# Moving the statistics, norms and transposes of four token tiles between groups of matmuls

## The chip, the cores and the metric

The kernel runs on one core of a Trainium2 chip. The core has engines with instruction queues of their own, each worked off strictly in order: TensorE (matrix multiplies; PE in the profile, its weight loads PEld), VectorE (DVE), ScalarE (ACT), GpSimd (POOL) and SyncE (SP), which here only issues DMAs. They meet through semaphores: an instruction waits until a producer on another engine, or a DMA, has counted up. The metric is the device time of one execution in microseconds (us), as the median of several runs.

## The reference

A transformer block in bf16 on x of 2048 tokens by 1024: a layer norm, a linear attention with 32 heads, an output projection and a residual; then a second layer norm, a gated FFN with a hidden width of 3584, and a residual.

```python
n  = layernorm(x)                       # no scale, no bias, eps 1e-5
q, k, v = split(n @ wqkv)               # 32 heads of 32
phi = lambda t: where(t > 0, t + 1, exp(t)) + 1e-6
kv  = einsum("hsd,hse->hde", phi(k), v) # sums over all tokens
z   = einsum("hsd->hd", phi(k))
o   = (phi(q) @ kv) / (phi(q) @ z + 1e-6)
h   = x + o @ wo
m   = layernorm(h)
out = h + (relu(m @ W_gate) * (m @ W_up)) @ W_down
```

The change lies in the first stage: layer norm, k, v and the sums over tokens.

## The kernel before

**Tiles.** The 2048 tokens are 16 tiles `st` of 128. In turn a tile is loaded (`load_x1`, into a ring of four places, so tile 8 takes the place of tile 4, tile 12 that of tile 8), gets its mean and variance, is normalised on VectorE (`ln1_norm`: line 970, or 914 for tiles whose statistics came from VectorE), and is transposed by a DMA on SP (`T1d`, issued at line 641) into `xnT`, where the contracted dimension lies on the partitions. `T1d(st)` issues the load of tile st + 4 behind its transpose; `T1d(st, False)` doesn't.

**Two ways to the statistics.** `ln1_stats` and `ln1_steps` run on VectorE: two `bn_stats` (line 859), one aggregate (864), one add (868), then a power on POOL (871). `ln1_steps` returns these as four steps. `ln1_stats_act` runs on ScalarE with accumulating activations (line 885): a mean over 1024 elements, and squares, which come as two halves, `q0` and `q`; small steps on POOL follow each (891, 900, 906, 909). In the code `m6, q6a, q6b` are the mean and the two halves for tile 6, and `m9`, `late_q` hold those of later tiles until a place calls them.

**Groups of seven products.** Pairs of tiles are multiplied by a fast scheme of the Strassen-Winograd kind (`sgroup`): the 2 by 2 blocks of tokens and contraction, times the 2 by 2 blocks of contraction and output columns, take seven products of four 128x128x512 matmuls in place of eight. It needs sums of weight blocks (`w_sums`, line 1068, queues `twk`, `twv`, `twq`) and, for each pair p of tiles, four sums of its transposed blocks, `x_sums(p)` (line 1093, results Sx3, Sx1, Sx2, Sx4 in this order). The order in a group is P1, P7 (uses Sx3), P6 (Sx2), P2, P5 (Sx1), P4, P3 (Sx4). ScalarE copies the first bank of a product to a second one to be added to (`fk1` behind P1, for P6; `fk2` behind P6, for P5; all at line 850) and keeps two banks as `s7` and `sc`. A k group applies phi to its results: an exp on ScalarE (925), two steps on VectorE (929, 932), for two of the four blocks with a sum before (1187). A v group copies two blocks on ScalarE (1254) and sums two on VectorE (1248).

The groups run in the order k0, v2, k1, v3, k2, v4, k3, ...: `k_group(p)` and then `v_group(p + 2)`, where the number is the pair of tiles (v of pairs 0 and 1 comes from single products, `v_piece`, at the start). So v4 needs `x_sums(4)`, of tiles 8 and 9. Between P7 and P6 of k1 and k2, and before P3 of the later v groups, stand the small matmuls that sum over tokens (`kvacc`).

**What sets the order.** Nothing plans at run time: the program is written out in one order, and each engine's queue is its share of that order. `sgroup` calls `hook(i)` at seven places: 1 behind P1 and `fk1`, 2 behind P7, 3 behind P6 and `fk2`, 4 behind P2, 5 behind P5 (in v2 before the sum of that place, elsewhere behind it), 6 behind P4, 7 at the end. A hook first runs what the group before left in `pend[i]` (the rest of its phi, or its sums) and then the function that the caller gave. For k groups these come from `kv_hooks` and the loop at line 2353, for v groups from `v3`, `v5`, `v6`, `v7` at lines 2366 to 2409, where p is 0 for v2, 1 for v3, 2 for v4.

In the kernel before, the mean of tile 6 (`m6`) is called between two single products ahead of k0, its first half square (`q6a`) at k0's hook 3, its second at v2's hook 5, where tiles 6 and 7 are also normalised and transposed, with the loads of tiles 10 and 11 behind. Tile 8 gets its statistics at v3's hook 2 and its norm and transpose at hook 3; tile 9 its norm and transpose at hook 5.

Of the kernel before, what the change touches and what calls it, by code (L numbers as in the profile page):

```python
# [132 lines left out]
def bass_sequential_preLN__linear_attn_block__glu_gated_reglu__prompt_kernel(  # L133
# [71 lines left out]
    with es:  # L205
# [6 lines left out]
        NX1 = 4  # L212
# [423 lines left out]
        def dma(slot, dst_ap, src_ap, name, reads=(), writes=(), eng="sp"):  # L636
            return PL.add(eng, lambda e: e.dma_start(dst_ap, src_ap), reads=reads, writes=writes, slot=slot,  # L637
                          name=name)
# [5 lines left out]
        def load_x1(st, split=False):  # L644
            i = st % NX1
            if split:
                for c in range(NBC):
                    dma(sl_x1h[c], x1[:, i, c * BCH:(c + 1) * BCH], xv[st * P:(st + 1) * P, c * BCH:(c + 1) * BCH],
                        "ld_x1_%d_%d" % (st, c), writes=[B_x1[i][c]], eng=("sp", "act")[c])
            else:  # L650
                dma(sl_x1[i], x1[:, i, :], xv[st * P:(st + 1) * P, :], "ld_x1_%d" % st, writes=B_x1[i])
# [224 lines left out]
        def ln_stats(src_full, src_chunk_bufs, name):  # L876
            k, steps = ln_stats_steps(src_full, src_chunk_bufs, name)
            for f_ in steps:
                f_()
            return k  # L880
# [69 lines left out]
        def ln1_stats(st):  # L950
            i = st % NX1
            ln1_k[st] = ln_stats(x1[:, i, :], B_x1[i], "ln1_%d" % st)

        def ln1_steps(st):
            i = st % NX1
            ln1_k[st], steps = ln_stats_steps(x1[:, i, :], B_x1[i], "ln1_%d" % st)
            return steps

        def ln1_stats_act(st, split=False):
            i = st % NX1  # L960
            k = len(ln1_a) % 3
            ln1_a[st] = k
            return act_stats(x1[:, i, :], B_x1[i], xn[:, st % NXN, :], B_xn[st % NXN], s1[:, k, :], B_s1[k],
                             "ln1_%d" % st, split)

        def ln1_norm(st):
            i = st % NX1
            if st in ln1_a:
                k = ln1_a[st]
                PL.add("dve", lambda e: e.tensor_scalar(out=xn[:, st % NXN, :], in0=x1[:, i, :], scalar1=s1[:, k, 0:1],  # L970
                                                        scalar2=s1[:, k, 2:3], op0=ALU.subtract, op1=ALU.mult),
                       reads=B_x1[i] + [B_s1[k][0], B_s1[k][2]], writes=[B_xn[st % NXN]], name="ln1_%d_norm" % st)
            else:
                ln_norm_dve(ln1_k.pop(st), x1[:, i, :], B_x1[i], xn[:, st % NXN, :], B_xn[st % NXN], "ln1_%d" % st)
            if st in (2, 3):
                load_x1(st + NX1)
# [36 lines left out]
        def T1d(st, load=True):  # L1013
            k = st % NXN
            dma_t(sl_tx[k], xnT[:, :, st * P:(st + 1) * P], xn[:, k, :], "T1d_%d" % st, reads=[B_xn[k]],
                  writes=B_xnT[st])
            if load and st + NX1 < NST:
                load_x1(st + NX1)
# [36 lines left out]
        def v_copy(b, st, j):  # L1055
            sc, rd = (1.0, []) if st >= 2 else (rstd[:, v_k[st], :], [B_rstd[v_k[st]]])
            PL.add("act", lambda e: e.activation(out=v_out(st, j), in_=gw(bank(b)), func=ACTF.Identity, scale=sc),  # L1057
                   reads=[B_bank[b]] + rd, writes=[B_v[st % NV][j]], name="v_%d_%d" % (st, j))
# [22 lines left out]
        def x_sums(p, part=None):  # L1081
            def xb(k, t):
                st = 2 * p + t
                return xnT[:, k * KH:(k + 1) * KH, st * P:(st + 1) * P]

            def s(i):
                return Sx(i)[:, :, p * P:(p + 1) * P]

            def bx(k, t):
                return [B_xnT[2 * p + t][k]]  # L1090

            def add(i, in0, in1, op, reads):
                PL.add("dve", lambda e: e.tensor_tensor(out=s(i), in0=in0, in1=in1, op=op), reads=reads,  # L1093
                       writes=[B_Sx[i][p]], name="Sx%d_%d" % (i + 1, p))

            if part != 1:
                add(2, xb(0, 0), xb(0, 1), ALU.subtract, bx(0, 0) + bx(0, 1))
            if part == 0:
                return
            add(0, xb(0, 1), xb(1, 1), ALU.add, bx(0, 1) + bx(1, 1))  # L1100
            add(1, s(0), xb(0, 0), ALU.subtract, [B_Sx[0][p]] + bx(0, 0))
            add(3, xb(1, 0), s(1), ALU.subtract, [B_Sx[1][p]] + bx(1, 0))
# [72 lines left out]
        pend = {}  # L1175
# [1115 lines left out]
        T1d(4)  # L2291
        m6, q6a, q6b = ln1_stats_act(6, True)
        v_piece(3, 0)
        m6()
        twv.pop(0)()
        ln1_norm(5)
        T1d(5)
# [3 lines left out]
        b31 = v_piece(3, 1, copy=False)  # L2301
# [4 lines left out]
        def kv_hooks(p, nq):  # L2306

            sq = []
            A, B = 2 * p + 6, 2 * p + 7

            def k1():
                if p > 1 and A < NST:
                    ln1_stats(A)
                for _ in range(nq[0]):
                    twq.pop(0)()

            def k5():
                if p < 2:
                    x_sums(p + 2)
                elif p + 2 < NP_:  # L2320
                    x_sums(p + 2, 0)
                if p == 0:
                    m_, q0_, q_ = ln1_stats_act(B, True)
                    m_()
                    sq.extend([q0_, q_])
                while p == 1 and m9:
                    m9.pop(0)()
                while p > 0 and len(late_q) > (p == 1):
                    late_q.pop(0)()

            def k6():
                if p == 0:
                    twv.pop(0)()
                elif 1 < p < NP_ - 2:
                    x_sums(p + 2, 1)
            return {1: k1, 5: k5, 6: k6}, sq

        def norm(st):
            if st < NST:
                ln1_norm(st)  # L2340
                T1d(st)

        def norms(p):
            norm(2 * p)
# [8 lines left out]
        for p in range(NP_):  # L2353
            nq = NQ.get(p, (0, 0))
            hooks, sq = kv_hooks(p, nq)
            if p == 0:
                hooks[1], hooks[3] = lambda: v_copy(b31, 3, 1), q6a
            if p == NP_ - 1:
                hooks[7] = lambda: kvaccs(NP_ - 2)
            if p in (1, 2):  # L2360
                hooks[2] = lambda p=p: kvaccs(p - 1)
            k_group(p, hooks)
            if p + 2 < NP_:
                late = []

                def v3(p=p, sq=sq, late=late):
                    if p == 0:
                        x_sums(1)
                        return
                    if p == 1:  # L2370
                        late_q.pop(0)()
                    norm(2 * p + 6)
                    if 2 * p + 9 < NST:
                        m_, q0_, q_ = ln1_stats_act(2 * p + 9, True)
                        late += [m_, q_]
                        if p == 1:
                            late.append(q0_)
                        else:
                            q0_()

                def v5(p=p, sq=sq, late=late):
                    if p == 0:
                        for f_ in [q6b] + sq:
                            f_()
                        ln1_norm(6)
                        T1d(6, False)
                        ln1_norm(7)
                        T1d(7, False)
                        load_x1(6 + NX1)
                        load_x1(7 + NX1)  # L2390
                        return
                    norm(2 * p + 7)
                    for f_ in late[2:]:
                        f_()
                    if late:
                        late[0]()
                        late_q.append(late[1])

                def v6(p=p, nq=nq):
                    if p > 1:  # L2400
                        kvaccs(p)
                    for _ in range(nq[1]):
                        twq.pop(0)()

                def v7(p=p):
                    if p == 0:
                        m_, q0_, q_ = ln1_stats_act(9, True)
                        m9.append(m_)
                        late_q.extend([q0_, q_])
                vh_ = {3: v3, 5: v5, 6: v6, 7: v7}  # L2410
                if p == 1:
                    vh_[2] = lambda: ln1_stats(8)
                v_group(p + 2, vh_)
        assert not twq and not twv and not twk
        for i in range(ND2):
# [2 lines left out]
        for r in range(2):  # L2418
            for ct in range(NG // 2):
                hooks = {}  # L2420
# [268 lines left out]
```

## Time and profile before

| what | before |
|---|---|
| median of three runs | 715.29 us (714.87 to 715.64) |
| the profiled execution | 714.91 us, of which the span from first to last instruction is 713.1 us |
| TensorE busy | 707.2 us, 99% of the span |
| VectorE, ScalarE, POOL busy | 606.4, 411.5, 141.6 us |
| granted TensorE clock | 1.000 |
| x tile load by SP, issue to landing | 4.0 us (median) |
| DMA transpose of a tile (line 641), issue to landing, 8 to 130 us | 2.7 / 3.7 / 7.7 us (least, median, most) |

Times inside the execution are counted from the span's start. In a line of the timeline the columns are start, duration, engine, source line, operation, tiles written and read, shape, count, and in brackets the idle time of the engine before it and what ended it. In a line of waits they are who waited, for whom, the total, the number and the longest. In the chain of the work that ended last they are start, duration and what.

### The profile page before, as it was taken

Reading aid. Unit: us, or ns where it says so; the run is one execution under the profiler, and the core shown is the slowest. Engines: PE = TensorE matmul, PEld = TensorE weight load, DVE = VectorE, ACT = ScalarE, POOL = GpSimd, SP = SyncE. Lnnn points to the kernel's source line nnn. Section 1 sums busy time; section 2 is a strip of 40 time slices with the busy share of each in tenths; the row PEclk is TensorE's granted clock in tenths of the full one; section 3 lists DMA queues with packets and bytes.
Section 4 is the critical chain, followed back from the end, with each engine's and each line's share of the span. In section 5 each row is a group of like instructions: output and inputs, shape, how many; then the busy total and the mean of one; then the engine's idle time right before and its main releaser. Section 6 shows DMA issues by size and latency. Waiting matters only on the chain.

```text
span 713.1 us, 13262 instructions
## 1 busy us (share of the span) xinstructions
PE 707.2 (99%) x5039; PEld 392.8 (55%) x5039; DVE 606.4 (85%) x974; ACT 411.5 (58%) x741; POOL 141.6 (20%) x206
## 2 busy tenths in 40 slices
PE   9999999999999999999999999999999999999998
PEld 4443444444444455555554658865555555547887
DVE  6988867899878899999998787888889888988985
ACT  4897756764973687878786411046666767633010
POOL 3221100114983223132312001310000000000331
PEclk9999999999999999999999999999999999999999
DMA  9863245114999799999897989995343544267997
GB/s 297 262 99 82 33 115 167 44 30 93 236 195 286 224 333 304 317 249 297 260 296 238 279 241 321 313 222 161 97 133 111 149 116 127 76 206 256 320 316 188
DMA packets 195104, 144.21 MB, mean 202 GB/s; under 512 B 53984, under 2 KB 172512, under 8 KB 195040
## 3 DMA queue, kind: packets, MB, share of 16 engines
q1 hardware_dynamic: 190048, 138.77, 67.2%
q0 software_dynamic: 4032, 3.67, 3.6%
q10 hardware_dynamic: 960, 0.92, 0.4%
q8 instruction: 40, 0.66, 0.4%
q14 instruction: 24, 0.20, 0.1%
HBM read 98.76 MB, written 32.51 MB: 184 GB/s over the span
## 4 chain that ended last, share of the span: by engine, by line
PE 92%; DMA 3%; DVE 1%; issue 1%; ACT 1%; SPq 0%; POOL 0%; DVEq 0%; POOLq 0%
PE ps L845 92%; DMA RAB<-RXH 2%; DMA RE<-in_A_x_dram 1%; ACT RXH L885 1%; SPq L637 0%; DVE RWG L1093 0%; DVE RE L1971 0%; DVE st L859 0%; DVE RXH L970 0%; ACT RE L1057 0%; DVE RWG L1911 0%; DVE RE L1248 0%; DVE RX L1187 0%; ACT RX L850 0%; POOL s L909 0%
## 5 line engine op out<-in xcount | busy, mean ns | idle before, releaser
L850 ACT ACTIVATE ps<-ps 128x512 f32<-128x512 f32 (+1 forms) x263 | 133.1, 517 | 181.4 <-PE ps L845 137.1
L845 PE MATMUL ps<-RC,RO 128*128 128x512 f16 x616 | 147.0, 370 | 0.0
L845 PEld LDWEIGHTS ps<-RC,RO 128*128 128x128 f16 x616 | 60.0, 98 | 53.2 <-ACT ps L850 1.2
L850 ACT ACTIVATE RE<-ps 128x512 f32<-128x512 f32 (+3 forms) x106 | 63.8, 627 | 32.1 <-PE ps L845 18.0
L845 PE MATMUL ps<-RC,RWG 128*128 128x512 f16 x320 | 81.1, 380 | 0.7 <-ACT ps L850 0.6
L845 PE MATMUL ps<-RH,RWG 128*128 128x512 bf16 (+1 forms) x348 | 77.7, 349 | 0.0
L1980 POOL DMA_DIRECT2D out_dram<-RX x20 | 17.9, 1258 | 271.5 <-DVE RX L1971 218.4
L845 PE MATMUL ps<-RH,RO 128*128 128x512 bf16 (+1 forms) x256 | 65.3, 380 | 0.0
L1710 DVE TENSOR_TENSOR RE<-ps,RE 128x1024 bf16<-128x1024 f32 (+1 forms) x42 | 44.0, 1047 | 18.2 <-PE ps L845 18.1
L845 PE MATMUL ps<-RW,RAB 128*128 128x256 f16 (+3 forms) x374 | 56.0, 303 | 0.0
L845 PEld LDWEIGHTS ps<-RH,RWG 128*128 128x128 bf16 x348 | 33.9, 98 | 35.3 <-ACT ps L850 0.2
L845 PE MATMUL ps<-RAB 128*128 128x512 bf16 (+3 forms) x250 | 52.9, 349 | 0.0
L845 PEld LDWEIGHTS ps<-RC,RWG 128*128 128x128 bf16 (+1 forms) x320 | 30.0, 98 | 34.6 <-ACT ps L850 5.8
L845 PEld LDWEIGHTS ps<-RW,RAB 128*128 128x128 f16 (+1 forms) x374 | 36.4, 98 | 16.2 <-DVE RAB L1422 0.5
L1971 DVE TENSOR_TENSOR RE<-ps,RE 128x512 f32<-128x512 f32 x44 | 30.2, 687 | 14.4 <-PE ps L845 11.8
L1710 DVE TENSOR_TENSOR RAB<-ps,RE 128x1024 bf16<-128x1024 f32 x28 | 34.2, 1223 | 7.3 <-PE ps L845 6.6
L1722 ACT ACTIVATE RAB<-RAB 128x1024 bf16<-128x1024 bf16 x28 | 29.5, 1053 | 18.9 <-DVE RAB L1710 18.9
L1710 DVE TENSOR_TENSOR RAB<-RAB,RE 128x1024 bf16<-128x1024 bf16 x56 | 37.3, 686 | 3.1 <-ACT RE L850 2.8
L1576 DVE TENSOR_TENSOR RO<-RWG 128x1024 f16<-128x1024 bf16 x54 | 38.9, 721 | 0.0
L845 PEld LDWEIGHTS ps<-RH,RO 128*128 128x128 f16 (+1 forms) x256 | 24.4, 98 | 24.6 <-ACT RX L850 1.5
L1576 DVE TENSOR_TENSOR RO<-RWG,RO 128x1024 f16<-128x1024 bf16 x54 | 37.8, 700 | 0.0
L845 PEld LDWEIGHTS ps<-RAB 128*128 128x128 bf16 (+1 forms) x250 | 24.3, 98 | 21.9 <-ACT RAB L988 0.3
(212 smaller groups left out, 1294.8 us busy)
## 6 DMA issues: line engine op xcount, KB each, us to landing
RWG<-in_B_W_gate_dram SPq DMA_DIRECT2D x28, 512.0 KB, 5.6
RWG<-in_B_W_up_dram SPq DMA_DIRECT2D x28, 512.0 KB, 5.0
RW<-l_scr SPq DMA_DIRECT2D x20, 448.0 KB, 5.4
RW<-in_B_W_down_dram SPq DMA_DIRECT2D x14, 512.0 KB, 6.3
t_scr<-RW SPq DMA_DIRECT2D x14, 512.0 KB, 4.4
l_scr<-RX SPq DMA_DIRECT2D x7, 1024.0 KB, 7.9
RE<-l_scr SPq DMA_DIRECT2D x15, 448.0 KB, 5.4
RW<-t_scr SPq DMA_DIRECT2D x13, 448.0 KB, 5.6
```

The source lines that it names most:

```text
L845: lambda e: e.matmul(out_ap, lhsT, rhs, start=start, stop=stop, skip_group_check=skip),
L850: PL.add("act", lambda e: e.activation(out=dst, in_=src, func=func), reads=reads, writes=writes, name=name)
L885: PL.add("act", lambda e: e.activation(out=junk[:, c0:c1], in_=src[:, c0:c1], func=func, scale=scale, accum_out=sv[:, col:col + 1]), reads ...
L1576: PL.add(eng, lambda e: e.tensor_tensor(out=tb(j, u), in0=f0(u), in1=f1(u), op=ALU.subtract), reads=[B_w[i + x] for x in r] + ([B_T[k + x] ...
L1710: PL.add("dve", lambda e: e.tensor_tensor(out=dst, in0=in0, in1=in1, op=op), reads=reads, writes=writes, name=name)
L1722: PL.add("act", lambda e: e.activation(out=d, in_=d, func=ACTF.Relu), reads=[], writes=db, name=name)
L1971: PL.add(eng, lambda e: e.tensor_tensor(out=dst, in0=in0, in1=in1, op=op), reads=reads, writes=writes, name=name)
L1980: PL.add("pool", lambda e: e.dma_start(dst, src, accum_op=ALU.add), reads=[bsrc], writes=[B_hscr[st]], slot=sl, name="acc_%d_%d" % (st, dh))
```

## The change

It moves existing work to other places of the written order; no arithmetic is changed or left out. `m6` goes from ahead of k0 to k0's hook 5, in front of tile 7's mean, and `q6a` from k0's hook 3 to v2's hook 3. Tile 8's statistics go from v3's hook 2 to v2's hook 5: the two `bn_stats` between norms 6 and 7, the aggregate and the rest behind the loads of tiles 10 and 11. Tile 8's norm and transpose go from v3's hook 3 to its hook 2; tile 9's from the function at hook 5 into the list `pend[5]`, between the exp and the two VectorE steps of k1's last phi. The loads of tiles 12 and 13, each of which stood behind its transpose (8 and 9), now follow at v3's hook 5, behind both.

```diff
@@ -2291,7 +2291,6 @@
         T1d(4)
         m6, q6a, q6b = ln1_stats_act(6, True)
         v_piece(3, 0)
-        m6()
         twv.pop(0)()
         ln1_norm(5)
         T1d(5)
@@ -2320,6 +2319,7 @@
                 elif p + 2 < NP_:
                     x_sums(p + 2, 0)
                 if p == 0:
+                    m6()
                     m_, q0_, q_ = ln1_stats_act(B, True)
                     m_()
                     sq.extend([q0_, q_])
@@ -2335,10 +2335,10 @@
...
-        def norm(st):
+        def norm(st, load=True):
             if st < NST:
                 ln1_norm(st)
-                T1d(st)
+                T1d(st, load)
...
@@ -2354,7 +2354,7 @@
...
             if p == 0:
-                hooks[1], hooks[3] = lambda: v_copy(b31, 3, 1), q6a
+                hooks[1] = lambda: v_copy(b31, 3, 1)
...
@@ -2365,11 +2365,13 @@
 
                 def v3(p=p, sq=sq, late=late):
                     if p == 0:
+                        q6a()
                         x_sums(1)
                         return
                     if p == 1:
                         late_q.pop(0)()
-                    norm(2 * p + 6)
+                    if p > 1:
+                        norm(2 * p + 6)
...
@@ -2384,12 +2386,21 @@
                             f_()
                         ln1_norm(6)
                         T1d(6, False)
+                        s8 = ln1_steps(8)
+                        s8[0]()
+                        s8[1]()
                         ln1_norm(7)
                         T1d(7, False)
                         load_x1(6 + NX1)
                         load_x1(7 + NX1)
+                        s8[2]()
+                        s8[3]()
                         return
-                    norm(2 * p + 7)
+                    if p > 1:
+                        norm(2 * p + 7)
+                    if p == 1:
+                        load_x1(2 * p + 6 + NX1)
+                        load_x1(2 * p + 7 + NX1)
...
@@ -2409,7 +2420,8 @@
                 vh_ = {3: v3, 5: v5, 6: v6, 7: v7}
                 if p == 1:
-                    vh_[2] = lambda: ln1_stats(8)
+                    vh_[2] = lambda: norm(8, False)
+                    pend[5].insert(1, lambda: norm(9, False))
                 v_group(p + 2, vh_)
```

## The prediction

> **What bounds the kernel now.** I read the page first (busy times, then the chain that ended last), then TensorE's waits, then the timeline of each engine from 19 to 64 us, where every edit lies.
>
> ```profile
> PE 92%; DMA 3%; DVE 1%; issue 1%; ACT 1%; SPq 0%; POOL 0%; DVEq 0%; POOLq 0%
> ...
> PE ps L845 <- POOL RXH L618: 1.4, 1, 1.4
> PE ps L845 <- DVE RWG L1093: 0.9, 2, 0.4
> PE ps L845 <- ACT ps L850: 0.6, 1, 0.6
> ...
> 58.13 615.17 PE ps L845 x4316
> ```
>
> The chain is TensorE, from 58.13 us on 615 us of it without a break. So a microsecond that TensorE gains before 58 us comes out at the end, unless something new stops it. Its waits in the whole run are three: the start, one on ScalarE, two on VectorE's `x_sums` (L1093). Their places, in the timeline of TensorE:
>
> ```profile
> 23.17 1.03 PE L845 MATMUL ps<-RC,RWG 128*128 128x512 f16 x4
> 24.76 1.04 PE L845 MATMUL ps<-RC,RWG 128*128 128x512 f16 x4 [0.56 <-ACT ps L850]
> ...
> 55.21 1.03 PE L845 MATMUL ps<-RAB 128*128 128x512 bf16 x4
> 56.65 1.04 PE L845 MATMUL ps<-RW,RWG 128*128 128x512 f16 x4 [0.41 <-DVE RWG L1093]
> 58.13 1.02 PE L845 MATMUL ps<-RW,RWG 128*128 128x512 f16 x4 [0.45 <-DVE RWG L1093]
> 59.00 1.03 PE L845 MATMUL ps<-RAB 128*128 128x512 bf16 x4
> ```
>
> A product of four matmuls shows 1.03 us, but products without a wait start 0.87 us apart (58.13 to 59.00), as the last matmul's end overlaps the next. I therefore measure a stall from start to start, less 0.87: k0's P6 loses 24.76 - 23.17 - 0.87 = 0.72; v4's P7 loses 0.57 and its P6 0.61. A fourth shows only this way: in k1, P7 starts at 36.18 and P6, behind two `kvacc`, at 37.95, 1.77 apart, where k2 (49.29 to 50.89) takes 1.60: 0.17. Together 2.07 us is all that could be had here.
>
> The other two engines around them:
>
> ```profile
> 23.07 1.05 ACT L885 ACTIVATE RXH<-RE 128x1024 bf16<-128x1024 bf16 x1
> 24.02 0.20 ACT L885 ACTIVATION_READ_ACCUMULATOR RXH<-RE 128x1 f32 x1
> 24.11 0.59 ACT L850 ACTIVATE ps<-ps 128x512 f32<-128x512 f32 x1
> ...
> 28.66 0.68 DVE L1187 TENSOR_TENSOR RX<-ps,RX 128x512 f32<-128x512 f32 x1
> 29.36 0.77 DVE L1093 TENSOR_TENSOR RWG<-RAB 128x512 f16<-128x512 bf16 x2
> ...
> 50.59 1.24 SPq L641 DMA_TRANSPOSE RAB<-RXH  x1
> ...
> 56.17 0.42 DVE L1093 TENSOR_TENSOR RWG<-RAB 128x512 f16<-128x512 bf16 x1 [1.10 <-DMA RAB<-RXH]
> ```
>
> The mean of tile 6 (23.07) stands before the fork copy `fk1` (24.11) that k0's P6 waits for. VectorE has no idle time at all from 22.08 to 37.7. And the transpose of tile 9, issued at 50.59, lands at 56.15 (5.56 us), which is what VectorE and, through it, v4 wait for.
>
> **Edit 1: mean and squares of tile 6.** *k0.* P1 ends at 23.17 + 0.16 = 23.33, so with the mean (1.04 us to the next start) gone `fk1` runs 23.43 to 24.01 and P6 starts at 24.07, behind P7 (24.04): the 0.72 is gone, less 0.03. The half square `q6a` (0.61) goes from behind `fk2` as well, so `sc` follows P5 as before. k0 now ends 0.69 earlier and v2's P1 starts at 28.46.
> *Who pays.* ScalarE does the mean at 27.5 in front of tile 7's mean: 2 x 1.04 ends at 29.55, and v2's `fk1` is wanted at 29.59 (P1's end 29.49 + 0.10); before, 1.02 us idle stood there. `q6a` goes into 0.67 us idle before v2's `sc` (33.79); 0.61 fits. On POOL the 0.59 of the mean's L891 goes into 4.43 us idle.
> *What is late next.* v2's P7 needs the first result of `x_sums(2)`, Sx3. VectorE reaches that at 29.36 by its own queue (weight sums until 27.73, the two steps of a phi at 27.73 and 28.05, a sum at 28.66) and tile 5's transpose lands there too (issued 25.69, 3.7 later). Nothing of that moves. Its result is ready at 29.78, the weights load at 29.84, so P7 starts at 29.86 instead of 30.00: 0.14 is left of 0.69. In k1, `fk1` stands behind tiles 6's and 7's squares, and these behind VectorE's sum (34.09): that chain starts at `fk2` of v2, moves 0.11, and so k1's P6 starts at 37.84. **Gain of edit 1: 0.11 us**, not 0.72. Were VectorE not full, it would be 0.72 + 0.17.
>
> **Edit 2: statistics of tile 8 into v2.** VectorE does two `bn_stats` (1.32, 45.48 to 46.80) after norm 6, which starts at 37.07; norm 7 starts at 38.80 instead of 38.56 (0.81 us idle, waiting for POOL, absorbs most) and ends at 39.35. The aggregate and the add (0.24 + 0.15) follow, then v2's two sums (2 x 0.60), the three steps of k1's phi and its sum: 39.27, 39.6, 40.2, 40.83, 41.15, 41.76, and `x_sums(3)` at 42.36 instead of 42.19. Tile 7's transpose is issued at 39.38 instead of 39.13; it took 3.03 to land (42.16), so 42.41. v3's P7 wants it done at 43.09 (43.20 - 0.11): 42.43 + 0.42 + 0.06 = 42.91. **Cost 0**, with 0.18 us to spare. k1's `sc` (40.70) needs the first sum read (40.3): it is. In v3 the 1.65 us of statistics are gone from VectorE.
> The bound: a transpose between 23 and 64 us landed after 2.7 to 5.56 us. At 2.7 VectorE's own 42.36 decides; at 5.56, P7 would start at 45.44, 2.35 late. I take 3.03, the same pair with the same loads behind it. "DMA: Bandwidth & Descriptors" (section "Latency and other measured facts") gives a DMA transpose 261 GB/s; for a tile of 256 KB that is an estimate of 1.0 us of moving, and by it, behind the issue, the cost would be 0 as well.
>
> **Edit 3: norms and transposes of tiles 8 and 9 sooner.** In v3 VectorE reaches hook 2 at 45.6 (before: `bn_stats` at 45.48). Norm 8 (0.54) goes there, transpose 8 is issued at 46.2 instead of 48.60. Norm 9 needs POOL's power: `q_9` on ScalarE ends at 46.7, and POOL's three steps no longer stand behind tile 8's power (47.28, 0.56), so it is ready at 47.6. VectorE is there at 48.05, after v3's sum that waits for `sc`; transpose 9 issues at 48.6 instead of 50.59, and the load of tile 12 (0.57 of SP's queue) no longer stands between. Landing by 51.6 (3.03) to 54.2 (5.56). Behind norm 9 VectorE holds k1's last phi and v3's second sum; they come at 48.5 to 49.4, 0.6 to 1.1 earlier than before.
> `x_sums(4)` is then set by VectorE: k2's exp, phi and sum (53.45, 53.78, 54.39, less 0.11) end in `x_sums(4, 0)` at 54.88, in place of 56.17. v4's P7 at 55.97 finds it (55.30); the three others, behind a sum at 55.26, give Sx2 for P6 at 56.72, and `fk1` ends at 56.81, so P6 starts at 56.87. Against 58.13 that is 1.26, of which 0.11 was edit 1's: **edit 3 gains 1.15 us**.
> The loads of tiles 12 and 13 are issued at about 49.9 and 50.4 (before 49.89 and 51.93); their first readers come at 63.91 and 61.51. Free.
> A rule against this edit stands in "SBUF — State Buffer" (section "SBUF: two separate sides"): a GpSimd operation that reads SBUF is blocked while VectorE runs one with two SBUF inputs. Here POOL's power (L871) took 1.48 us beside a weight sum at 14.02 and 0.55 to 0.78 elsewhere. With 1.48, norm 9 would come 0.5 later and its transpose land by 54.7 at the worst, still before 54.88: same sum.
>
> **Sum.** 0.11 + 0 + 1.15 = 1.26 us. The profiled execution took 714.91 us (span 713.1 and 1.81 around it), so 713.65 for it; the median of the three runs stands 0.38 above, so **714.0 us**, 0.18% faster. No change can be told from one of about 0.2% (1.43 us) here.
>
> **Rivals.**
> *More is gained (15%).* All 2.07 us go, or more, if tile 9's transpose costs the unprofiled runs more than the profiled one, which is the 0.38 above: 713.2. For it: the runs spread over 0.77 us. Against all 2.07: 27.73 to 29.36 on VectorE.
> *Half is gained (12%).* `x_sums(4)` or another step in v4 is late for a new reason: at 0.6 us of 1.15 the time is 714.6. For it: v4's P6 has 0.15 us between Sx2 and its start. Against: VectorE idles 0.67 and 1.10 us in k2.
> *Slower (8%).* Tile 7's transpose lands late behind the two `bn_stats`, and v3's P7 waits. The place has 0.18 us to spare, so from 3.2 us on it costs, from 4.5 us on it eats the 1.26. At 5.56 us v3 waits 2.35 and the time is 716.4; at 7.7, the longest landing in all of this line's rows, 718.5. Against it: 3.03 for this very transpose.
> *The forecast (65%)*: 714.0, and 713.4 to 714.7 for itself, by the 0.4 us to which the runs before stand around their median and 0.2 us for the slacks of 0.15 and 0.18.
>
> **How the numbers follow.** The range runs from the first rival with 0.1 beyond it (713.1) to 715.2, which takes in the half gain and a wait of 1.2 us in v3; beyond lie some 6 in 100 of the slow rival, the lower tail of the first, and what I did not see. The forecast's centre is 0.17 us from the bound at 713.86, so about 0.30 of its 0.65 lies beyond it; with the first rival 0.45 for faster. Slower than 716.72 takes a landing of tile 7 over 5.9 us (39.38 + 5.9 + 0.5 is 45.78, 2.69 late), or a wait in a place that I did not see: 0.07. The rest, 0.48, is within.
>
> **What would show it.** After: TensorE's wait on L850 gone, but a wait on L1093 or a later start of the weight load at v2's P7 near 29.86; k1's P6 near 37.84; tile 8's and 9's transposes issued near 46.2 and 48.6; `x_sums(4)` not waiting for a DMA; TensorE's unbroken stretch starting near 56.9. Wrong: k0's 0.69 arriving whole in v4, a wait at v3's P7, or a new wait after 64 us.

## The result, and the profile after

| | before | after |
|---|---|---|
| median of ten runs, us | 715.56 (714.87 to 715.90) | 713.79 (713.34 to 714.22) |
| the profiled execution, us | 714.91 | 713.63 |
| its span, us | 713.1 | 711.9 |

The ratio is 0.9976, with a 95% interval from 0.9967 to 0.9986: 0.24% or 1.8 us less, and between 1.0 and 2.4 us by the interval. The forecast of 714.0 us stood 0.21 us above the median, and the measured 1.28 us between the two profiled executions stand beside a predicted 1.26.

The waits of TensorE, and then the longest step of the chain that ended last, in the changed kernel:

```profile
PE ps L845 <- POOL RXH L618: 1.4, 1, 1.4
PE ps L845 <- DVE RWG L1093: 0.4, 1, 0.4
PE ps L1006 <- DVE RXH L997: 0.2, 1, 0.2
PE ps L845 <- ACT ps L850: 0.2, 1, 0.2
...
37.87 634.24 PE ps L845 x4466
```

Of the 0.6 us on ScalarE 0.2 are left, in another place (k1), and one of the two waits on VectorE is gone. The 0.2 us on L997 lie in the opening, before 9 us and ahead of every edit. TensorE runs unbroken from 37.87 us instead of 58.13. Where the one wait on `x_sums` stands now is read in the timeline of TensorE:

```profile
23.24 1.89 PE L845 MATMUL ps<-RC,RWG 128*128 128x512 f16 x8
...
28.46 1.03 PE L845 MATMUL ps<-RAB 128*128 128x512 bf16 x4
29.90 1.91 PE L845 MATMUL ps<-RW,RWG 128*128 128x512 f16 x8 [0.41 <-DVE RWG L1093]
...
36.05 1.03 PE L845 MATMUL ps<-RC,RWG 128*128 128x512 f16 x4
37.87 1.04 PE L845 MATMUL ps<-RC,RWG 128*128 128x512 f16 x4 [0.15 <-ACT ps L850]
...
42.26 1.03 PE L845 MATMUL ps<-RAB 128*128 128x512 bf16 x4
43.17 1.91 PE L845 MATMUL ps<-RW,RWG 128*128 128x512 f16 x8
...
55.20 1.03 PE L845 MATMUL ps<-RAB 128*128 128x512 bf16 x4
56.06 1.93 PE L845 MATMUL ps<-RW,RWG 128*128 128x512 f16 x8
57.84 1.03 PE L845 MATMUL ps<-RAB 128*128 128x512 bf16 x4
```

k0's P7 and P6 are one group of eight at 23.24: the stall of 0.72 is gone. It comes back as v2's P7, which starts 1.44 behind P1 in place of 0.87. From start to start, less 0.87 for each four matmuls, the losses after are 0.57 in v2 (28.46 to 29.90), 0.22 in k1 (36.05 to 37.87 is 1.82, where 1.60 is free), 0.04 in v3, and 0.04 in v4 (56.06 to 57.84 is 1.78, where two products take 1.74): 0.87 us together. Before, the four places came to 2.07. The difference, 1.20 us, is as large as the change of the span. Nearly all of it is v4: its P1 starts at the same time as before (55.20 against 55.21), its P2 1.16 us sooner (57.84 against 59.00).

What makes v4 sooner stands on SyncE and VectorE. The timeline of SyncE and then of VectorE, in the changed kernel:

```profile
46.38 3.54 SPq L641 DMA_TRANSPOSE RAB<-RXH  x2
49.97 1.06 SPq L637 DMA_DIRECT2D RE<-in_A_x_dram  x2
...
42.69 0.76 DVE L1093 TENSOR_TENSOR RWG<-RAB 128x512 f16<-128x512 bf16 x2 [0.36 <-DMA RAB<-RXH]
...
54.98 0.42 DVE L1093 TENSOR_TENSOR RWG<-RAB 128x512 f16<-128x512 bf16 x1
```

Transposes 8 and 9 are issued from 46.38 on, the loads of tiles 12 and 13 behind both, and `x_sums(4)` at 54.98 waits for no DMA. How long tile 9's transpose took from issue to landing, in the trace of before and then of after:

```profile
L641 SPq DMA_TRANSPOSE RAB<-RXH x1: 1241/1241/1241, 50.6 to 50.6; - x1
...
DMA to landing us min/median/max: 5.6/5.6/5.6
```

```profile
L641 SPq DMA_TRANSPOSE RAB<-RXH x1: 1233/1233/1233, 48.7 to 48.7; - x1
...
DMA to landing us min/median/max: 2.8/2.8/2.8
```

The issue moved by 1.9 us, and the landing shortened by another 2.8. The data were there at about 51.5, some 3.5 us before VectorE asked for them. That is far more than was needed, and it opens the question for the experiments: which of the moves pays.

### The profile page after: what moved, and what is told of

Read it like the earlier page. It is cut to its first block, busy times and chain, and to the rows that moved or that the text cites. A ratio compares the mean times of both kernels' runs of the same rounds, so it can differ in the third digit from the quotient of the medians.

```text
span 711.9 us, 13262 instructions
## 1 busy us (share of the span) xinstructions
PE 706.8 (99%) x5039; PEld 393.2 (55%) x5039; DVE 605.5 (85%) x974; ACT 411.9 (58%) x741; POOL 141.8 (20%) x206
## 4 chain that ended last, share of the span: by engine, by line
PE 94%; ACT 1%; DVE 0%; issue 0%
PE ps L845 94%; ACT RXH L885 0%; DVE RE L1971 0%; DVE RWG L1911 0%; ACT RX L925 0%; ACT RX L850 0%; ACT ps L850 0%; ACT RE L1254 0%; DVE RX L1971 0%
## 5 line engine op out<-in xcount | busy, mean ns | idle before, releaser
L850 ACT ACTIVATE ps<-ps 128x512 f32<-128x512 f32 (+1 forms) x263 | 133.1, 517 | 179.9 <-PE ps L845 135.8
L845 PEld LDWEIGHTS ps<-RC,RO 128*128 128x128 f16 x616 | 60.1, 98 | 53.1 <-ACT ps L850 1.2
L850 ACT ACTIVATE RE<-ps 128x512 f32<-128x512 f32 (+3 forms) x106 | 63.8, 627 | 32.1 <-PE ps L845 18.0
```

The lines of the kernel that those rows point to most:

```text
L845: lambda e: e.matmul(out_ap, lhsT, rhs, start=start, stop=stop, skip_group_check=skip),
L850: PL.add("act", lambda e: e.activation(out=dst, in_=src, func=func), reads=reads, writes=writes, name=name)
```

## The experiments

All kernels compute everything that the reference does. Ratios are to the kernel before on the same chip, with 95% intervals. Its median was 715.49 us beside the first four, 715.63 beside the second four and 715.44 beside the last three.

| kernel | median, us | ratio |
|---|---|---|
| before, with edit 1 alone | 715.36 | 0.9999 (0.9991 to 1.0008) |
| after, without edit 1 | 713.99 | 0.9979 (0.9970 to 0.9988) |
| before, only the two loads behind both transposes | 713.92 | 0.9977 (0.9968 to 0.9987) |
| after, the load of tile 12 again between the transposes | 713.73 | 0.9975 (0.9966 to 0.9984) |
| before, with edit 2 alone | 714.41 | 0.9983 (0.9974 to 0.9992) |
| after, a weight sum behind `x_sums(2)` | 715.25 (one run) | |
| before, unchanged | 715.71 | 1.0002 (0.9993 to 1.0010) |
| before, norm 9 a product later | 715.05 | 0.9992 (0.9983 to 1.0001) |
| after, a weight sum on POOL | 714.96 | 0.9993 (0.9984 to 1.0002) |
| before, thirty short opening matmuls | 715.73 | 1.0005 (0.9996 to 1.0014) |
| after, thirty short opening matmuls | 714.93 | 0.9994 (0.9985 to 1.0003) |

### Edit 1 alone, and everything but edit 1

Edit 1 put into the kernel before:

```diff
         v_piece(3, 0)
-        m6()
         twv.pop(0)()
...
                 if p == 0:
+                    m6()
                     m_, q0_, q_ = ln1_stats_act(B, True)
...
-                hooks[1], hooks[3] = lambda: v_copy(b31, 3, 1), q6a
+                hooks[1] = lambda: v_copy(b31, 3, 1)
...
                     if p == 0:
+                        q6a()
                         x_sums(1)
```

> Edit 1 alone on the kernel before. Theory (VectorE and the squares eat it): k0's P6 follows P7 without a stall, v2's P7 then waits about 0.4 us on L1093 and starts near 29.9, k1's P6 gains 0.1 us at most, v4's two stalls (0.57 and 0.61 us) stay: time within 0.2 us of before, 715.4. Rival (edit 1 carries the part of the measured 1.8 us that the two profiles, 1.2 us apart, don't show): 0.6 us faster, ratio 0.9992 or less.

The other kernel is the change with these edits undone.

> Edits 2 and 3 without edit 1. Theory: k0's P6 stalls 0.72 us as before, v4 has no stall, and the time is that of the full change to 0.1 us (ratio to before 0.9976 to 0.9984). Rival (edit 1 carries a third of the gain): about 0.6 us slower than the full change, ratio 0.9985 to 0.999.

The waits of TensorE with edit 1 alone, and then the four places of its timeline at which it waits on VectorE:

```profile
PE ps L845 <- DVE RWG L1093: 2.0, 4, 0.8
...
29.91 1.91 PE L845 MATMUL ps<-RW,RWG 128*128 128x512 f16 x8 [0.38 <-DVE RWG L1093]
...
43.66 1.91 PE L845 MATMUL ps<-RW,RWG 128*128 128x512 f16 x8 [0.37 <-DVE RWG L1093]
...
57.50 1.04 PE L845 MATMUL ps<-RW,RWG 128*128 128x512 f16 x4 [0.78 <-DVE RWG L1093]
58.98 1.02 PE L845 MATMUL ps<-RW,RWG 128*128 128x512 f16 x4 [0.44 <-DVE RWG L1093]
```

The stall in k0 is gone in this kernel too, v2's P7 waits at 29.91 and v3's at 43.66, and v4 loses 1.55 us (1.18 in the trace of before, 1.61 in that of its repeat further down). The time is that of before. The change without edit 1 has k0's stall again (P6 at 24.89 waits 0.52 for L850), no wait at v2's P7 and none in v4, a loss of 0.33 us at v3's P7, and the time of the full change: 713.99 against 713.79. So edit 1 contributes nothing that these runs can tell, and what the traces show as gained is gained in v4.

### The order of the loads alone

The kernel before, with norms and statistics where they were; the loads of tiles 12 and 13 follow both transposes:

```diff
-        def norm(st):
+        def norm(st, load=True):
...
-                T1d(st)
+                T1d(st, load)
...
-                    norm(2 * p + 6)
+                    norm(2 * p + 6, p > 1)
...
-                    norm(2 * p + 7)
+                    norm(2 * p + 7, p > 1)
+                    if p == 1:
+                        load_x1(2 * p + 6 + NX1)
+                        load_x1(2 * p + 7 + NX1)
```

> The kernel before with one difference: the loads of tiles 12 and 13 follow both transposes of tiles 8 and 9; norms and statistics stay where they were. Theory of the prediction (the norms have to come 2 us sooner): the transpose of tile 9, issued near 50.6, still lands near 56.1, v4 stalls 1.18 us, time as before. Rival (it is the load in front of the transpose in SP's queue that makes it land after 5.6 us): it lands after 2.8 us near 53.4, x_sums(4) starts near 55.0 without waiting for a DMA, and 1.1 to 1.2 us are gained with no norm moved.

SyncE, VectorE and TensorE in the timeline of this kernel:

```profile
49.17 3.21 SPq L641 DMA_TRANSPOSE RAB<-RXH  x2
52.43 1.26 SPq L637 DMA_DIRECT2D RE<-in_A_x_dram  x2
...
55.22 0.41 DVE L1093 TENSOR_TENSOR RWG<-RAB 128x512 f16<-128x512 bf16 x1
...
56.31 1.93 PE L845 MATMUL ps<-RW,RWG 128*128 128x512 f16 x8
```

Tile 9's transpose is issued near 51.1, half a microsecond later than in the profile of before, and all the same `x_sums(4)` finds it. It landed after 3.7 us, near 54.8; that is neither the 5.6 of the theory nor the 2.8 of the rival. v4's P7 and P6 run as one group of eight. The time is that of the full change, with no norm and no statistics moved. The prediction's reason, that the norms have to come two microseconds sooner, is therefore not needed for the gain.

### The norms sooner, with a load between the transposes again

The change, with the load of tile 12 put back behind transpose 8:

```diff
-                        load_x1(2 * p + 6 + NX1)
                         load_x1(2 * p + 7 + NX1)
...
-                    vh_[2] = lambda: norm(8, False)
+                    vh_[2] = lambda: norm(8)
```

> The full change, but the load of tile 12 again between the transposes of tiles 8 and 9 on SP. Both theories: x_sums(4) is reached by VectorE near 55.0 and the transpose of tile 9, issued near 48.7, has landed by 54.3 at the latest, so the time is that of the full change to 0.1 us. What tells them apart is the landing: 5.6 us if the load in front is the cause, 2.8 us as in the full change if it is not.

SyncE and VectorE in the timeline of this kernel:

```profile
46.32 1.23 SPq L641 DMA_TRANSPOSE RAB<-RXH  x1
47.61 0.57 SPq L637 DMA_DIRECT2D RE<-in_A_x_dram  x1
48.64 1.23 SPq L641 DMA_TRANSPOSE RAB<-RXH  x1
49.97 0.52 SPq L637 DMA_DIRECT2D RE<-in_A_x_dram  x1
...
54.92 0.41 DVE L1093 TENSOR_TENSOR RWG<-RAB 128x512 f16<-128x512 bf16 x1
```

The gain is whole. The order on SyncE is that of before, and yet tile 9's transpose lands after 3.3 us. A load in front is thus not by itself what makes 5.6 us of it, and the norms sooner are a second way to the same gain.

### The statistics alone

The kernel before with edit 2 alone:

```diff
+                        s8 = ln1_steps(8)
+                        s8[0]()
+                        s8[1]()
                         ln1_norm(7)
...
                         load_x1(7 + NX1)
+                        s8[2]()
+                        s8[3]()
                         return
...
-                if p == 1:
-                    vh_[2] = lambda: ln1_stats(8)
```

> Edit 2 alone: tile 8's statistics in v2, its norm and transpose at v3's hook 3 with the loads as before. Theory (cost 0): norm 7 starts 0.2 us later, v3's P7 waits 0 to 0.2 us, and v3's VectorE is 1.65 us emptier, so norm 8 comes about 1.2 us sooner; the gain then hangs on tile 9 alone, whose norm waits for POOL at 47.6 and for its place at hook 5: transposed from about 48.7 on, 2 us after tile 8's, and landed before 55. So a gain of 1.0 to 1.2 us if the landing is under 5.6 us. Rival (the norms' places in the program matter and not only the statistics): tile 9 is not sooner, v4 stalls 1.2 us, time as before.

SyncE, VectorE and TensorE in the timeline of this kernel:

```profile
47.77 1.23 SPq L641 DMA_TRANSPOSE RAB<-RXH  x1
...
50.07 1.23 SPq L641 DMA_TRANSPOSE RAB<-RXH  x1
...
55.02 0.43 DVE L1093 TENSOR_TENSOR RWG<-RAB 128x512 f16<-128x512 bf16 x1
...
56.10 1.93 PE L845 MATMUL ps<-RW,RWG 128*128 128x512 f16 x8
```

With 1.3 us of `bn_stats` out of VectorE's queue in v3, both norms come sooner by themselves. Tile 9's transpose lands after 4.9 us, near 55.0, just when VectorE asks. 1.2 us of 715.63 are gained: a third way. The measured 1.2 and the full change's 1.8 are not apart by their intervals.

### What holds v2's P7

The prediction said that edit 1's gain stops at v2's P7 because VectorE is full, with tile 5's transpose landing at the same time. This kernel is the change with one weight sum (1.22 us) taken from in front of `x_sums(2)` and put behind it:

```diff
-        twv.pop(0)()
...
+                    if p == 0:
+                        twv.pop(0)()
```

> The full change with one weight sum of v (1.2 us on VectorE) moved behind x_sums(2) in k0's hook 5. Theory (VectorE and tile 5's transpose set the same time at v2's P7): without that sum VectorE reaches x_sums(2) near 28.3, and it then starts when tile 5's transpose has landed, 25.8 + 3.6 = 29.4, as in the full change: P7 near 29.9 again. Rival (VectorE alone): x_sums(2) starts near 28.3 and P7 at 29.3, behind P1. In both P6 waits for the moved sum, which ends near 32, so the time is 0.5 to 1.3 us worse than the full change.

VectorE and TensorE in its timeline, a single execution:

```profile
29.17 0.77 DVE L1093 TENSOR_TENSOR RWG<-RAB 128x512 f16<-128x512 bf16 x2 [1.11 <-DMA RAB<-RXH]
...
28.24 1.03 PE L845 MATMUL ps<-RAB 128*128 128x512 bf16 x4
29.65 1.04 PE L845 MATMUL ps<-RW,RWG 128*128 128x512 f16 x4 [0.38 <-DVE RWG L1093]
32.13 1.02 PE L845 MATMUL ps<-RW,RWG 128*128 128x512 f16 x4 [1.45 <-DVE RW L1068]
```

VectorE is now there 1.1 us early and waits for tile 5's transpose until 29.17. Up to here this execution runs some 0.2 us ahead of the full change: v2's P1 starts at 28.24 in place of 28.46, and P7 at 29.65 in place of 29.90. From P1 to P7 it is 1.41 us against 1.44, so 1.2 us less on VectorE are worth 0.03 at this place, as the theory said. In the trace of the full change tile 5's transpose lands at 29.39 and VectorE takes up `x_sums(2)` at 29.42. The two bounds thus coincide, and the one run shows that taking away VectorE's alone does not help. The sum that was put off is then missed by P6, which waits 1.45 us for it.

### The same sum on POOL

The obvious way to free VectorE is to give a weight sum to POOL, which is busy a fifth of the span. This kernel is the change with one weight sum of v (128x1024) on POOL, k's last sum put ahead of norm 5, and the loads of tiles 8 and 9 behind transpose 5, so that this lands sooner:

```diff
-        def w_sums(wsrc, bw, tw, btw, name, chunk, cw=NW):
+        def w_sums(wsrc, bw, tw, btw, name, chunk, cw=NW, eng="dve"):
...
-                    PL.add("dve", lambda e: e.tensor_tensor(out=t(j)(d), in0=in0(d), in1=in1(d), op=ALU.subtract),
+                    PL.add(eng, lambda e: e.tensor_tensor(out=t(j)(d), in0=in0(d), in1=in1(d), op=ALU.subtract),
...
+        twv[1] = w_sums(wv_, bw_v, tw_v, B_TWv, "TWv", KH // 2, eng="pool")[2]
...
```

> The full change with 0.65 us less on VectorE ahead of v2: one weight sum of v (1024 elements) on POOL near 19.7, the weight sum of k ahead of norm 5, and the load of tile 8 behind tile 5's transpose instead of ahead of it. Theory (VectorE and tile 5's transpose bound v2's P7 and P6): P7's wait of 0.57 goes, P6 starts near 30.4 instead of 30.77, k1's P6 0.3 to 0.5 us sooner; of that at most 0.4 us comes through, tile 7's transpose permitting: ratio to before 0.997 to 0.9976. Rival (POOL's sum takes VectorE's port and slows it by as much, or tile 7's transpose gives it back at v3's P7): time of the full change or up to 0.5 us worse.

POOL, VectorE and TensorE in its timeline:

```profile
19.93 2.33 POOL L1068 TENSOR_TENSOR RW<-RAB 128x1024 f16<-128x1024 bf16 x1
...
20.32 2.23 DVE L1093 TENSOR_TENSOR RWG<-RWG,RAB 128x512 f16<-128x512 f16 x1
...
25.54 1.02 PE L845 MATMUL ps<-RC,RWG 128*128 128x512 f16 x4 [0.97 <-DVE RC L1068]
```

While POOL's sum runs, from 19.93 to 22.26, a sum of VectorE that takes 0.42 to 0.43 us in the traces of before and after takes 2.23, and ends 0.29 behind it. VectorE lost 1.8 us where it was to be relieved of 0.65. k0's P6 now waits 0.97 us for a weight sum, and the kernel is 1.2 us slower than the full change, more than the 0.5 that the rival allowed. The Trainium skill, "SBUF — State Buffer" (section "SBUF: two separate sides"), says that VectorE's instructions with two inputs in SBUF and GpSimd's share a port pair as an exclusive lock held for a whole instruction, and that the other one fully blocks; these two rows agree.

### Before once more, and norm 9 later

To see how steady tile 9's late landing is, the kernel before was run again unchanged.

> The kernel before, unchanged, to see what two samples of the same kernel differ by and how steady the landing of tile 9's transpose is. Theory (the landing follows from the order on SP): 5.6 us again and v4's stalls within 0.3 us of 1.18; ratio 1.000 with an interval of about 0.001. Rival (a chance late landing in the one profile): another landing, 3 to 4 us, and no stall in v4.

VectorE and TensorE in its timeline:

```profile
56.87 0.43 DVE L1093 TENSOR_TENSOR RWG<-RAB 128x512 f16<-128x512 bf16 x1 [1.52 <-DMA RAB<-RXH]
...
43.46 1.91 PE L845 MATMUL ps<-RW,RWG 128*128 128x512 f16 x8 [0.35 <-DVE RWG L1093]
57.36 1.04 PE L845 MATMUL ps<-RW,RWG 128*128 128x512 f16 x4 [0.83 <-DVE RWG L1093]
58.84 1.02 PE L845 MATMUL ps<-RW,RWG 128*128 128x512 f16 x4 [0.45 <-DVE RWG L1093]
```

The transpose again took 5.6 us. It was issued at 51.21 rather than 50.59. v4 loses 0.4 us more than in the first trace, a little beyond the 0.3 that the theory allowed; v3's P7 loses 0.5, where the first trace shows nothing, and k0's P6 0.4 less. The span is 713.8 us, 0.7 above the execution that the prediction was made on.

In the next kernel norm 9, with its transpose and load, stands at v3's hook 6 in place of 5:

```diff
-                    norm(2 * p + 7)
+                    if p > 1:
+                        norm(2 * p + 7)
...
+                    if p == 1:
+                        norm(2 * p + 7)
```

> The kernel before with tile 9's norm, and with it its transpose and the load of tile 13, one place LATER: behind v3's second sum, so the transpose is issued near 51.2, some 1.3 us behind the load of tile 12 in place of 0.7. Theory of the prediction (sooner is better, 5.6 us to land): landing near 56.8, v4 stalls 0.6 us more, ratio 1.0009. Rival (the long landing comes from a transpose issued 0.7 us behind a load): landing after 3.3 us or less, near 54.5, before VectorE asks for it at 55, and the whole gain of 1.1 us by a step in the wrong direction: ratio 0.998.

The median is 715.05, and the ratio doesn't tell it from before. Its transpose 9 is issued at 51.85, 0.64 later than in the repeat of before, and lands after 4.7 us, 0.9 sooner than there. `x_sums(4)` waits 1.18 for it, until 56.58. Theory and rival were both wrong here: a transpose issued later landed sooner, but not after 3.3 us. Neither the issue time nor the order on SyncE sets the landing alone.

### Is it the instruction fetch?

In the DMA view of before, the engines' busy tenths in 40 slices of 0.2 us from 48.6 us on, and what one microsecond in the gap held:

```profile
DMA  0000009999906972799999920000000099996700
...
q8 instruction: 1, 0.02, 5.8%
```

The same of the kernel after, from 46.3 us on:

```profile
DMA  0000004999920000009999909913899997100000
```

In before, the DMA engines work on transpose 8 and the load from 49.8, on transpose 9 until about 53.3, stand almost still for 1.6 us, and then finish. In the gap falls one fetch of instructions, 16 KB on a queue of its own, at 53.27. In the trace's DMA records, where the packets of a transpose (256 bytes) mostly take 18 ns, twenty that start between 52.7 and 53.1 take 2.0 to 2.3 us. The fetch comes in each kernel at some time from 51.8 to 55.2. Set against the issue of transpose 9:

| kernel | fetch, us behind the issue of transpose 9 | its landing, us |
|---|---|---|
| before, its repeat, edit 1 alone | 2.7 | 5.6 |
| edit 2 alone | 1.8 | 4.9 |
| norm 9 later | 0.95 | 4.7 |
| before with short opening matmuls | 0.4 | 4.8 |
| loads behind both transposes | 0.8 | 3.7 |
| load between, norms sooner | 4.1 | 3.3 |
| after, without edit 1, weight sum late, sum on POOL, after with short opening matmuls | 3.8 to 4.9 | 2.8 |

Inside the flight of the transpose: 3.7 to 5.6 us, in all seven kernels. Behind it: 2.8 to 3.3, in all six. The kernel with edit 2 alone and the one with a load between have the same order and spacing on SyncE (transposes 2.30 and 2.32 us apart) and differ by 1.7 us in the landing, so the order is not all of it.

The earlier transposes of the same thirteen traces part the two. Those of tiles 4 and 8, without a load shortly in front and without a fetch in their flight, land after 2.7 us in all thirteen. That of tile 6, with a fetch in its flight and no load shortly in front, takes 3.3 to 4.3 us. That of tile 5, with no fetch but a load in front, takes 3.6 to 3.75 us in twelve; in the kernel with the sum on POOL, where its loads stand behind it, 2.8.

To move the fetch by itself, the nine matmuls that open the kernel, which keep TensorE busy on zeros, were split into thirty of 128 columns, in before and in after. If the fetch is one of TensorE's instructions, 42 more of them (a matmul and a weight load each) bring it sooner:

```diff
-        def pe_dummies(n, banks):
+        def pe_dummies(n, banks, w=512):
...
-                mm(bank(b, 512), zeros_t[:, 0:P], zeros_t, True, True, [B_zeros], B_bank[b], "dummy")
+                mm(bank(b, w), zeros_t[:, 0:P], zeros_t[:, 0:w], True, True, [B_zeros], B_bank[b], "dummy")
...
-        pe_dummies(9, [KVB] + P1_POOL)
+        pe_dummies(30, [KVB] + P1_POOL, P)
```

> The kernel before with nothing moved in its stages; only the nine opening matmuls on zeros (512 columns) are thirty of 128 columns, so TensorE's queue is 42 instructions longer. In the trace of before a 16 KB instruction fetch (queue q8) starts at 53.27, in the middle of tile 9's transpose, whose packets then stand still until 55. Theory (the fetch is TensorE's and holds the transpose up): the fetch comes 42 instructions sooner, near 50.5 to 51, the transpose lands after 3.3 to 4 us, before VectorE asks for it at 55, v4's stalls are gone and 1.0 to 1.2 us are gained, ratio 0.998 to 0.9985. Rival (the load in front of the transpose does it, the fetch is a bystander): landing after 5.6 us, v4's stalls as before, ratio 1.000.

> The full change with the same thirty opening matmuls. Theory: the fetch (52.45 in the full change) comes near 50 to 50.5, in the middle of tile 9's transpose, which then lands after 4 to 4.7 us, near 53, still before VectorE asks at 55: time of the full change to 0.2 us. Rival (the load in front does it): landing 2.8 us as in the full change.

In before the fetch came some 2 us sooner relative to TensorE's k2, and tile 9's transpose landed after 4.8 us, between the 4 of the theory and the 5.6 of the rival; in after it came 0.6 later, not sooner. The opening itself also got 1.2 to 1.3 us longer (k0's P7 at 24.39 and 24.57), which hides any gain in the times. The pair decides nothing. That the landing grows when the fetch falls into it is what thirteen traces show; that the fetch is the cause is not shown. The held packets do not start at one time relative to it: 0.2 to 0.6 us before the fetch in before, but 0.9 us behind its start, where it is nearly over, in the kernel with the loads moved alone. The loads in flight add a part too: with a fetch inside, 3.7 us with the loads behind, against 4.7 to 5.6 with one in front.

## Why the prediction was right, and where its reason was not

**k0 and v2 (edit 1): right.** P6 follows P7 without a stall, v2's P7 was put at 29.86 and came at 29.90, waiting for L1093 as said. ScalarE's two means fitted before v2's `fk1`: it starts at 29.58, forecast 29.59. With `m6` out of the way VectorE's queue and tile 5's transpose bind together, 0.03 us apart, as the prediction had read from the trace of before.

**What edit 1 leaves: 0.11 predicted, about 0 measured.** k1's P6 came at 37.87 (forecast 37.84), 0.08 sooner than before. Then `x_sums(3)` waited for tile 7's transpose, and v3's P7 came at 43.17 where 43.09 was forecast and 43.20 was before. k2's P1 starts at 48.42 against 48.43. This term was mis-sized by 0.1 us.

**Edit 2: 0 predicted, 0.04 measured.** Norm 7 came at 38.77 (38.80 forecast), the two sums behind it at 39.53 and 40.13 (39.6 and 40.2). What came late was the issue of tile 7's transpose. SyncE's rows for the transposes of tiles 6 and 7 after the change, and VectorE's for norm 7:

```profile
L641 SPq DMA_TRANSPOSE RAB<-RXH x2: 1308/1708/2109, 37.7 to 39.8; - x2
...
DMA to landing us min/median/max: 2.8/3.1/3.5
...
38.77 0.53 DVE L970 TENSOR_SCALAR RXH<-RE,s 128x1024 bf16<-128x1024 bf16 x1
```

Norm 7 ends at 39.30, but SyncE is busy for 2.1 us with transpose 6, for which it took 1.23 in the trace of before, and issues transpose 7 at 39.84, where 39.38 was forecast. It landed after 2.8 us, sooner than the 3.03 that the prediction took, at 42.66. So the slack of 0.18 us went to SyncE, a step that the sum did not price, and not to the statistics. In eleven of the thirteen traces that issue of transpose 6 takes 2.0 to 2.6 us, in the repeat of before too; the one trace that the prediction had is one of the two with 1.23. Why it takes longer is not shown. The prediction named a wait at v3's P7 as a sign of being wrong, and its slower rival put one there, though by a late landing and at more than the 0.04 us that came.

**Edit 3: 1.15 predicted, 1.16 measured, by a broader cause.** The steps came nearly as written: norm 8 at 45.81 (45.6 forecast), transpose 8 at 46.38 (46.2), norm 9 at 48.13 (48.05), `x_sums(4)` at 54.98 (54.88), v4's P7 at 56.06 (55.97). POOL's power took 0.56 us, so the rule on the shared port made nothing of it here. TensorE's unbroken stretch was forecast from near 56.9 on and begins at 37.87, as v4 has no wait left. What was too narrow is the reason. The earlier issue, which the prediction counted on, is enough: with a load between the transposes again, the norms sooner still bring the whole gain. But it is not needed. The prediction wrote of the load of tile 12 that its "0.57 of SP's queue" stood between, and kept 5.56 us as an upper end of the landing. The kernel with the loads moved alone shows that their place is worth the whole gain, through the landing (3.7 us) and not through SyncE's queue, where transpose 9 is issued no sooner; the fetch also comes at another point of the flight there. The moved statistics do it as well. Every way has one end: tile 9's transpose lands before VectorE reaches `x_sums(4)` at 55.0. The change does all three and has 3.5 us to spare, so the three don't add up.

**The level: 714.0 against 713.79.** The prediction put the median 0.38 above the profiled execution. In ten runs of before it is 0.65 above, and the repeat of before shows a span 0.7 us longer, with 0.9 us more of stalls in v3 and v4 and 0.4 less in k0. After the change, the profiled execution (713.63) and the median (713.79) stand 0.16 apart. So the medians fell by 1.77 us where the sum had 1.26: the profiled execution of before was a short one. The first rival, more gained because tile 9's transpose costs the unprofiled runs more, probably had a part in it, and v3's stall another, at some 0.5 us of median together. That rests on one further profile; the stalls of the unprofiled runs can't be seen. Between the two profiled executions the 1.28 us measured and the 1.26 forecast agree in part by luck: at v4's P2 TensorE's timeline has gained 1.16, as edit 1's 0.1 did not come, and the other 0.12 came from outside the working.

**No new wait.** TensorE's wait on L850 that is left (0.2 us, in k1) stood there before too, without a mark. No wait of TensorE on another engine appeared behind 64 us, and the loads of tiles 12 and 13 were not missed.

## What to carry to other kernels

A stall that is taken away is worth what the next engine in line allows: 0.72 us on ScalarE was worth nothing that could be measured here, because VectorE was full and a transpose landed at the same time, and both could be read in the profile beforehand. Where a wait ends on a DMA, cost its landing and not only its issue, and look at what else is in the DMA queues while it flies; the cheapest way to the whole gain was two loads issued behind two transposes. A slack of 0.18 us read from one trace is not safe: the repeat of the same kernel issued that transpose 1.0 us later. Count the ways to one end once: three moves that each remove the same wait give one gain, and the rest is slack.

## What the runs showed of the hardware that was not expected

The same DMA transpose of 256 KB took 2.8 to 5.6 us to land in one place of one program, and in the trace of before, with 5.6, there is a stretch of about 1.6 us in the middle in which none of the DMA engines moves much. All seven cases over 3.5 us had a 16 KB fetch of instructions inside the flight and none of the six shorter ones had; whether the fetch holds the others up or is held up with them stays open. A load issued in front goes with a longer landing also where no fetch comes: tile 5's transpose took 3.6 to 3.75 us with one, and 2.8 in the one kernel without.

POOL's sum of 128x1024 took 2.33 us, and a sum of VectorE beside it 2.23 in place of 0.42: the idle engine was no free place for this work.
